# The opening of an attention-and-ReGLU kernel: chunk-wise loads of the keys' source, one form of line sums, and softmax row sums added ahead

## The chip, the cores and the metric

The kernel runs on one core of one Trainium2 chip. The metric is the device time of one execution in microseconds. Three runs of the kernel before took 1024.46, 1024.46 and 1024.63 us; their median is 1024.46 us.

## The reference, cut to what matters

```python
# q: (4, 12288, 128)   kv: (4, 384, 32, 128)   w_sr: (128, 128), all float32
kv_pool = kv.reshape(B, H // 4, 4, W // 4, 4, C).mean(axis=(2, 4))   # 4 x 4 pixels -> 1
k = v = kv_pool.reshape(B, -1, C) @ w_sr                             # 768 keys per image
s = (q @ k.transpose(0, 2, 1)) / sqrt(C)
a = exp(s - s.max(-1));  a /= a.sum(-1) + 1e-9
x = (a @ v).reshape(B * N, C)                                        # 49152 rows
out = (maximum(x @ w_gate, 0) * (x @ w_val)) @ w_out                 # d_ff = 1536
```

So each image has 768 pooled and projected keys, which are its values too, and each of the 12288 queries of an image goes through one softmax and one gated feed-forward layer. The two row-wise divisions by the softmax sum are left to the end: the feed-forward layer is of second degree in x, so its output is scaled by the inverse of the sum, squared.

## The kernel before

**Tiles.** The queries are cut into 96 tiles of 512 rows. The 768 keys of an image are six chunks of 128; two neighbouring chunks are a pair, because one row of the picture data holds both. A loaded line of a pair is a 128 x 1024 tile: 128 positions, and for each the four pixels of the even chunk and the four of the odd one, 4 KB together. Four such lines (one for each row of the 4 x 4 window) make a pair; six chunks are three pairs, 2 MB each.

**Steady part.** From the seventh tile on, one tile after another goes through the same written-out list of steps (`STEADY`): scores `s`, exponentials `e`, values `x`, value projections `v`, gate projections `g`, the gated product `h` and the output projection `o`. TensorE does s, x, v, g and o; ACT the exponentials and the copies `y` of the value projections out of PSUM; VectorE the gated products; GpSimd the output scaling. The next image's keys are prepared between these steps.

**Opening.** Image 0's keys must be made first, and meanwhile nothing of the steady kind can run. This part is a list of its own, `OPENING`, in which the order of the words is the order of issue on every engine (each engine works its own instructions off in that order). A number after `@` is the PSUM bank that a word takes. A dictionary `ENGINES` says which of ACT (a), VectorE (v) or GpSimd (p) does a word. The words that matter here:

- `a`, `b`, `c` with a chunk's number add loaded lines of a chunk (`sum_lines`, 128 x 512 fp32); the dictionary `SUMS` says which lines. `p` adds neighbouring pixels (128 x 256), `r` once more (128 x 128).
- `T3.2` transposes line 2 of chunk 3 on TensorE and adds it up in PSUM, four 128 x 128 fp32 matmuls (`turn_add`, L300); `T3.p` and `T3.r` do that with what `p` (two) or `r` (one) left. So a line may be summed on an engine ahead, or by TensorE itself.
- `kvT`, `pj`, `key`, `vt`, `val` copy the transposed chunk out, project it with w_sr (L314), keep the keys, transpose them into values (L329) and keep these.
- `cast`, `qt`, `qT` turn the first query tiles (L209). `S2.4` are the scores of tile 2 with chunk 4 (L378), `E2.4` their exponentials on ACT, `V2.4` the values (L456); `xT` keeps a finished sum of values as fp16.
- `U` with a list of chunks adds up the softmax sums of tiles 0 to 3 (`lead_sums`, L474): a matmul with ones for each tile and chunk, four tiles side by side. `R` turns these sums, `R2` inverts and squares them, `lsc` spreads them for the output scaling of `oT0`.
- `D0`, `D1` and `F384`, `F256` are matmuls whose result nobody reads; `fill(2)` at the very start is of the same kind (L663). `gate` holds GpSimd's queue until a line has landed, `W0`, `W1`, `wo` then load the weights, `ql4`, `ql5`, `qd` later queries.

**Loads before.** Pair 0's four lines go out on SP and ACT by turns, then on SP w_sr, two pairs of query tiles (512 KB each), the four lines of pair 1 and the four of pair 2. Of the eight latest loads on these two queues' shared set of semaphores, each is reused in turn: an issue waits until the load eight issues earlier has landed.

Of the kernel before, what the change touches and what calls it, by code (L numbers as in the profile page):

```python
# [16 lines left out]
def kernel(  # L17
# [33 lines left out]
    T = 512  # L51
    NS = T // 128
# [6 lines left out]
    LEAD = GRP  # L59
# [4 lines left out]
    assert NFB == 2 * NJC and NST % GRP == 0 and W // r == 8 and HC == 64  # L64

    ENGINES = dict(word.split(":") for word in """
        a0:v a1:v p0:v r0:v b1:v c1:v p1:v kvT0:v r1:p cast0:a cast1:a key0:v kvT1:v qT0:v
        cast2:a cast3:v qT1:v val0:v key1:v qT2:v qT3:v val1:a a2:v a3:v p2:p b3:v c3:v kvT2:a
        p3:p key2:a kvT3:a val2:v a5:v key3:v p5:v a4:v r5:v b4:v val3:a c4:v kvT5:a p4:v key5:v
        kvT4:a val5:v key4:v val4:v xT0:v xT2:v y0.8:v y0.2:a xT1:v y2.0:a y0.10:a cast4:p y0.7:a  # L70
        y0.6:a cast5:p y0.0:a y2.1:a xT3:a y0.1:a y1.10:a y0.5:a y0.4:a y0.3:a y0.9:a y1.8:a
        y1.1:a y1.0:a y0.11:a y1.11:v y1.3:a y2.3:a y1.7:a y1.4:a y2.2:a y2.7:a y2.4:a y1.5:a
        y1.6:a y1.2:a y2.5:v y1.9:a y2.6:a y2.11:a y2.8:a y2.9:a y2.10:a
    """.split())
    OPENING = """
        D1@2 D0@2 F384@2 a0 a1 p0 r0 T0.r@0 T0.3 b1 T0.2 c1 F256@2 p1 kvT0 r1 cast0 pj0@0 T1.r@1
        cast1 qt0@2 key0 kvT1 vt0@0 qT0 qt1@3 cast2 pj1@1 cast3 S0.0@2 qT1 qt2@4 E0.0 qt3@5 val0
        key1 qT3 S1.0@3 E1.0 vt1@1 val1 V0.0@2 S1.1@0 E1.1 S0.1@5 E0.1 qT2 S2.0@4 S2.1@1 V1.0@3
        a2 S3.1@6 V1.1 E3.1 V0.1 S3.0@5 T2.2@0 V3.1@6 p2 E2.1 a3 T2.p V2.1@1 E2.0 b3 T2.3 c3 E3.0
        U0.1@5 kvT2 pj2@0 V2.0 key2 p3 T3.p@4 kvT3 S2.2@0 E2.2 vt2@7 val2 V3.0 gate2.1 S1.2@4  # L80
        E1.2 pj3@7 a5 S0.2@0 V2.2 W0 key3 W1 ql4 ql5 S3.2@4 E0.2 E3.2 p5 V1.2 a4 S3.3@7 S0.3@0
        E3.3 V0.2 T5.2@4 E0.3 r5 T5.r vt3@7 val3 T5.3 kvT5 wo S1.3@0 S2.3@7 b4 c4 p4 V3.3 pj5@4
        V3.2 E1.3 T4.p@0 E2.3 V1.3 key5 vt5@4 S2.5@7 kvT4 val5 pj4@0 key4 E2.5 S0.5@4 E0.5 V0.3
        V2.3 S0.4@0 vt4@7 E0.4 V2.5 val4 S1.4@4 V0.5 E1.4 S2.4@7 V0.4 xT0 E2.4 S1.5@0 E1.5 S3.5@4
        V1.4 V2.4 E3.5 S3.4@7 qd3 xT2 v0.8@2 v0.2@0 E3.4 qd1 V1.5 y0.8 v0.10@4 y0.2 v2.0@1 qd0
        U2.3.4.5 xT1 y2.0 qd2 y0.10 cast4 v0.7@3 R v0.6@1 y0.7 g0.2@4 qT4 g2.0@0 h0.2 v0.0@2 y0.6
        v2.1@3 cast5 g0.7@5 h2.0 V3.5 y0.0 g0.6@4 v0.1@1 qT5 h0.7 V3.4 y2.1 v1.10@2 g0.10@0 h0.6
        xT3 o0.7@5 g0.1@3 y0.1 o0.2 h0.10 o0.6 y1.10 v0.5@4 h0.1 g0.0@1 g2.1@0 y0.5 v0.4@2 h0.0
        o0.10 y0.4 v0.3@3 g0.4@4 h2.1 o0.0 y0.3 g1.10@2 v0.9@1 h0.4 g0.5@0 y0.9 v1.8@3 h1.10 s4.0
        y1.8 o0.4 v1.1@1 h0.5 e4.0 g0.8@2 tq1 g0.9@3 h0.8 g1.8@4 v1.0@0 y1.1 o0.5 h1.8 qn1.8 s4.1  # L90
        y1.0 v1.11@2 g1.0@1 h0.9 e4.1 g0.3@4 v0.11@0 h1.0 o0.8 v1.3@3 y0.11 s4.2 y1.11 y1.3
        g1.1@1 v2.3@0 h0.3 o0.9 e4.2 g0.11@3 g2.2@2 h1.1 o0.1 y2.3 v1.7@4 o0.3 h0.11 v1.4@1 y1.7
        g1.7@0 s4.3 R2 y1.4 o0.11 h1.7 lsc e4.3 k5 g1.3@4 v2.2@1 h1.3 o1.0@3 v2.7@0 y2.2 o1.1 oT0
        o1.7 y2.7 g1.4@4 v2.4@1 h2.2 o1.3 y2.4 v1.5@0 v1.6@5 h1.4 g1.11@2 y1.5 g2.3@1 o1.8 h1.11
        y1.6 v1.2@0 g2.4@4 h2.3 s5.0 y1.2 v2.5@5 g2.6@2 h2.4 e5.0 v1.9@0 o1.10 y2.5 g2.5@1 y1.9
        g1.5@4 s5.1 h1.5 o1.4 e5.1 g1.2@0 v2.6@5 h2.5 g1.6@4 o1.11 y2.6 o1.5 h1.6 v2.11@1 s5.2
        h1.2 y2.11 o1.6 g2.7@4 e5.2 v2.8@5 h2.6 v2.9@0 g1.9@1 h2.7 o1.2 y2.8 g2.8@2 s5.3 h1.9
        y2.9 v2.10@5 g2.9@4 e5.3 h2.8 g2.11@0 o1.9 g2.10@1 h2.9 y2.10 oT1 h2.10 h2.11
    """.split()
    LAST = [f"{head}{n}" for n in range(NFB) for head in "ovygh"] + ["oT"]  # L100
    DRAIN = """
# [43 lines left out]
    def engine_of(name):  # L145
        return {"a": nc.scalar, "v": nc.vector, "p": nc.gpsimd}[ENGINES.get(name, "a")]
# [32 lines left out]
    def q_load_pair(i):
        q32 = work.tile([128, 2, NS, C], FP32, tag="kv_s2", bufs=2, name="q32")  # L180
        nc.sync.dma_start(
            q32, q[0, i * T : (i + 2) * T, :].rearrange("(p i s) c -> p i s c", i=2, s=NS)
        )
        for n in range(2):
            q32s[i + n] = q32[:, n]
# [40 lines left out]
    kv16 = const.tile([128, B, NJC, 2 * C + 16], FP16)  # L226
    kv_in = {}

    def kv_load(b, pair, lines=range(r), queues=(nc.sync,)):
# [12 lines left out]
        rows = kv[b, pair * 2 * HC : (pair + 1) * 2 * HC].rearrange(  # L242
            "(hp dh) (wp h dw) c -> dh hp wp (h dw c)", dh=r, h=2, dw=r
        )
        for dh in lines:
            queues[dh % len(queues)].dma_start(  # L246
                parts[dh].rearrange("p h dw c -> p (h dw c)"), rows[dh]
            )

    s3s, kv_Ts, key_banks = {}, {}, {}  # L250
# [15 lines left out]
    def line(chunk, dh):  # L266
        return kv_in[0, chunk // 2][dh][:, chunk % 2]

    sums, pixels = {}, {}

    def add(name, to, x, y):
        engine_of(name).tensor_tensor(to, x, y, op=ALU.add)  # L272
# [98 lines left out]
    aTs, x_banks, x16s, xTs, rinvs = {}, {}, {}, {}, {}  # L371
# [93 lines left out]
    sums_left = [NJC]  # L465

    def lead_sums(chunks):
        for jc in chunks:
            first = "sums" not in x_banks
            if first:  # L470
                x_banks["sums"] = bank([128, T])
            sums_left[0] -= 1
            for k in range(LEAD):
                nc.tensor.matmul(  # L474
                    x_banks["sums"][32 * k : 32 * (k + 1), :], ones, aTs[k][:, jc, :],
                    start=first, stop=sums_left[0] == 0, skip_group_check=True,
                    tile_position=(0, 32 * k),
                )

# [155 lines left out]
    ones = const.tile([128, 32], FP16)  # L635
# [40 lines left out]
    gate = const.tile([128, 1], FP32)  # L676

    def open_step(word):
        head = "T" if word[0] == "T" else word.rstrip("0123456789.")
        at = [int(x) for x in word[len(head):].split(".") if x] if head != "T" else []  # L680
        if head in ("a", "b", "c"):
            j = at[0]
            x, y = SUMS[j][head]
# [34 lines left out]
        elif head == "xT":  # L718
            lead_kept(word, at[0])
        elif head == "U":  # L720
            lead_sums(at)
        elif head == "R":
            lead_inverse() if at else lead_sums_turned()
        elif head == "lsc":
# [11 lines left out]
        elif head == "D":  # L736
# [3 lines left out]
                start=True, stop=True,  # L740
# [3 lines left out]
            nc.gpsimd.dma_start(wv16[:, own], moe_w_val[:, own])  # L744
            nc.gpsimd.dma_start(wg16[:, own], moe_w_gate[:, own])
        elif head == "gate":
            nc.gpsimd.tensor_copy(gate, line(2 * at[0], at[1])[:, 0, 0:1])
        elif head == "ql":
            q_load_tile(at[0])
        elif head == "wo":  # L750
# [1 line left out]
        elif head == "qd":  # L752
            q_tiles(1)
            rows = q[0, GRP * T : 2 * GRP * T, :].rearrange(
                "(i t j s) c -> j t i s c", i=GRP, t=32, s=NS
            )
# [12 lines left out]
        elif head == "o":  # L769
            k, n = at[0], o_left.get(at[0], NFB)  # L770
# [137 lines left out]
```

## Time and profile before

| what | before |
|---|---|
| median of three runs | 1024.46 us (1024.46 to 1024.63) |
| span of the profiled execution, first to last instruction | 1022.5 us |
| median time less that span | 1.96 us |
| TensorE (PE) busy | 1017.2 us, 99% |
| ACT busy | 918.5 us, 90% |
| VectorE (DVE) busy | 869.4 us, 85% |
| GpSimd (POOL) busy | 524.0 us, 51% |
| mean granted TensorE clock | 1.000 |

The profile has no time of its own for the profiled execution but the span: its own time is taken as the span with the 1.96 us around it. Rows of a timeline read: start, duration (for several merged instructions, from the first start to the last end), engine, line of the kernel, operation, tile written and tile read, shapes, count, and in brackets the idle time before it with what ended it. Rows of groups read: line, engine, operation, count, then total busy time and mean duration in ns, then the idle time before. A matmul's row includes its drain; the next one starts before it ends. Rows of stretches give the length, then busy time and count for PE, its weight loads, DVE, ACT and POOL, then the granted clock, the DMA share and GB/s.

### The profile page before, as it was taken

Reading aid. Unit: us, or ns where it says so; the run is one execution under the profiler, and the core shown is the slowest. Engines: PE = TensorE matmul, PEld = TensorE weight load, DVE = VectorE, ACT = ScalarE, POOL = GpSimd, SP = SyncE. Lnnn points to the kernel's source line nnn. Section 1 sums busy time; section 2 is a strip of 40 time slices with the busy share of each in tenths; the row PEclk is TensorE's granted clock in tenths of the full one; section 3 lists DMA queues with packets and bytes.
Section 4 is the critical chain, followed back from the end, with each engine's and each line's share of the span. In section 5 each row is a group of like instructions: output and inputs, shape, how many; then the busy total and the mean of one; then the engine's idle time right before and its main releaser. Section 6 shows DMA issues by size and latency. Waiting matters only on the chain.

```text
span 1022.5 us, 17480 instructions
## 1 busy us (share of the span) xinstructions
PE 1017.2 (99%) x5021; PEld 485.2 (47%) x5021; DVE 869.4 (85%) x1450; ACT 918.5 (90%) x1927; POOL 524.0 (51%) x1312
## 2 busy tenths in 40 slices
PE   9999999999999999999999999999999999999998
PEld 4444444444444444444444444444444444444445
DVE  5988888888888888888888888888888888888888
ACT  5999998999999999999999999999999999999986
POOL 3487857344437576544434856754434543443342
PEclk9999999999999999999999999999999999999999
DMA  9999999878799999868779999978787878777651
GB/s 317 172 171 184 186 211 145 140 122 132 132 198 156 201 164 184 136 116 143 125 134 201 165 186 187 157 131 137 128 130 114 147 122 129 124 119 124 98 91 44
DMA packets 475743, 153.48 MB, mean 150 GB/s; under 512 B 451584, under 2 KB 465920, under 8 KB 475648
## 3 DMA queue, kind: packets, MB, share of 16 engines
q1 hardware_dynamic: 453184, 126.08, 65.9%
q0 software_dynamic: 22032, 25.19, 17.6%
q10 hardware_dynamic: 432, 1.11, 0.3%
q8 instruction: 39, 0.64, 0.3%
q14 instruction: 56, 0.46, 0.2%
HBM read 53.94 MB, written 26.35 MB: 79 GB/s over the span
## 4 chain that ended last, share of the span: by engine, by line
PE 99%; DMA 1%; DVE 0%; ACTq 0%; issue 0%
PE bank_ps L504 24%; PE bank_ps L515 24%; PE bank_ps L545 24%; PE wide_ps L397 12%; PE bank_ps L439 12%; PE bank_ps L529 1%; DMA kv_in<-in_kv_dram 1%; PE bank_ps L456 1%; PE bank_ps L378 1%; PE wide_ps L336 0%; PE bank_ps L300 0%; PE bank_ps L314 0%; PE bank_ps L474 0%; DVE kv_s L272 0%; PE bank_ps L209 0%; ACTq L246 0%
## 5 line engine op out<-in xcount | busy, mean ns | idle before, releaser
L523 DVE SCALAR_TENSOR_TENSOR hT<-bank_ps,val 128x512 f16<-128x512 f32 x1152 | 727.3, 679 | 104.4 <-PE bank_ps L515 83.7
L141 ACT CAST val<-bank_ps 128x512 f16<-128x512 f32 x1149 | 628.4, 596 | 44.4 <-PE bank_ps L504 23.9
L504 PE MATMUL bank_ps<-xT,wv 128*128 128x512 f16 x1152 | 421.0, 379 | 0.0
L515 PE MATMUL bank_ps<-xT,wg 128*128 128x512 f16 x1152 | 376.3, 379 | 0.0
L545 PE MATMUL bank_ps<-hT,wo 128*128 128x512 f16 x1116 | 348.7, 379 | 0.0
L402 ACT ACTIVATE a<-wide_ps 128x768 f16<-128x768 f32 x368 | 302.2, 821 | 44.0 <-PE wide_ps L397 44.0
L397 PE MATMUL wide_ps<-kv,qT 128*128 128x512 f16 x736 | 179.8, 326 | 0.0
L439 PE MATMUL bank_ps<-aT,kv 128*128 128x512 f16 x552 | 179.0, 379 | 0.0
L558 POOL TENSOR_TENSOR o_sb<-o_t,scale 128x512 f32<-128x512 f32 x89 | 93.2, 1047 | 158.8 <-issue 141.0
L545 PEld LDWEIGHTS <-wo 128*128 128x128 f16 x1116 | 109.1, 98 | 132.1 <-issue 0.5
L515 PEld LDWEIGHTS <-wg 128*128 128x128 f16 x1152 | 112.6, 98 | 122.5 <-issue 0.2
L504 PEld LDWEIGHTS <-wv 128*128 128x128 f16 x1152 | 112.5, 98 | 105.4 <-issue 0.4
L423 POOL COPY scale<-square 32x8 f32<-32x8 f32 x736 | 141.2, 192 | 28.6
L416 POOL TENSOR_TENSOR square<-inverse 128x8 f32<-128x8 f32 x46 | 9.3, 202 | 248.9 <-DVE inverse L414 248.9
L838 POOL DMA_DIRECT2D out_dram<-o_sb x208 | 130.3, 632 | 9.6 <-POOL o_sb L558 7.4
L397 PEld LDWEIGHTS <-qT 128*128 128x128 f16 x736 | 71.9, 98 | 87.0 <-issue 0.2
L447 DVE CAST xT<-bank_ps 128x512 f16<-128x512 f32 x92 | 63.6, 691 | 31.7 <-PE bank_ps L439 31.6
L439 PEld LDWEIGHTS <-kv 128*128 128x128 f16 x552 | 53.9, 98 | 65.2
L402 ACT ACTIVATION_READ_ACCUMULATOR a<-wide_ps 128x1 f32 x368 | 76.1, 207 | 0.0
L553 DVE STREAM_TRANSPOSE o_t<-bank_ps 128x512 f32<-128x512 f32 x93 | 65.4, 703 | 0.3 <-PE bank_ps L504 0.2
L162 POOL DMA_DIRECT2D q<-in_q_dram x84 | 48.8, 581 | 0.3 <-issue 0.3
L256 POOL TENSOR_TENSOR s<-kv_in 128x512 f32<-128x512 f32 x36 | 45.1, 1281 | 0.7
(86 smaller groups left out, 210.8 us busy)
## 6 DMA issues: line engine op xcount, KB each, us to landing
kv_in<-in_kv_dram SPq DMA_DIRECT2D x42, 512.0 KB, 5.3
out_dram<-o_sb SPq DMA_DIRECT2D x177, 64.0 KB, 3.6
q<-in_q_dram POOLq DMA_DIRECT2D x88, 128.0 KB, 3.4
out_dram<-o_sb POOLq DMA_DIRECT2D x176, 64.0 KB, 4.2
aT<-a SPq DMA_TRANSPOSE x184, 4.5
kv_line<-in_kv_dram SPq DMA_DIRECT2D x4, 512.0 KB, 9.8
placed<-blocks SPq DMA_DIRECT2D x9, 128.0 KB, 2.5
kvT<-placed SPq DMA_DIRECT2D x36, 32.0 KB, 2.2
```

The costliest lines, as they stand in the source:

```text
L141: nc.scalar.copy(to, what)
L397: nc.tensor.matmul(s_ps[:, j0 * 128 : j1 * 128], qT, kv16[:, b, j0:j1, 0:C], start=True, stop=True)
L402: nc.scalar.activation(a16s[k][:, s, :], s_banks.pop(s)[:, 0:J], AF.Exp, scale=qk_scale, accum_out=a_sums[k // 2][:, k % 2, s : s + 1],)
L423: nc.gpsimd.tensor_copy(to[32 * b : 32 * (b + 1), :, :, j], squares[k // 2][32 * j : 32 * (j + 1)])
L439: nc.tensor.matmul(x_banks[k], kv16[:, k // NST, jc, C : 2 * C], aT[:, jc], start=first, stop=x_left[k] == 0,)
L504: nc.tensor.matmul(proj_banks["v", k, fb], wv16[:, fb * 128 : (fb + 1) * 128], xTs[k], start=True, stop=True,)
L515: nc.tensor.matmul(proj_banks["g", k, fb], wg16[:, fb * 128 : (fb + 1) * 128], xTs[k], start=True, stop=True,)
L523: nc.vector.scalar_tensor_tensor(hTs[k][:, fb, :], freed(proj_banks.pop(("g", k, fb))), 0.0, vals.pop((k, fb)), op0=ALU.max, op1=ALU.mult,)
L545: nc.tensor.matmul(o_banks[k], wo16[:, fb, :], hTs[k][:, fb, :], start=first, stop=o_left[k] == 0)
L553: nc.vector.transpose(o_t, freed(o_banks.pop(k)))
L558: nc.gpsimd.tensor_tensor(to, o_by, scale.to_broadcast([128, NS, 4, 32]), op=ALU.mult)
L838: queue.dma_start(*out_moves.pop())
```

## The change

1. **Loads.** A list `LOADS` takes the place of the six calls. Pair 0, w_sr and the first queries keep their queues and their order (of the two queues, ACT's first issue now stands first). Chunks 2, 3, 5 and 4 are then loaded one after the other, line by line, each line of a chunk by its own DMA: 128 pieces of 2 KB, 256 KB. `kv_load` gets a parameter `halves` for it.
2. **Line sums.** `SUMS` is the same for all six chunks: `a` adds lines 0 and 1, `b` adds line 2, TensorE transposes the sums' pixels (`T.p`) and the raw line 3 (`T.3`). The words `c` and `r` are gone.
3. **Row sums.** New words `m` (`m2.1`: for tile 2, chunk 2 + chunk 3) and `n` (`n2.1.2`: pair 1 + pair 2) add the fp16 exponentials ahead, six `m` on VectorE, six `m` and four `n` on GpSimd. `U6.7` then takes only two summed tiles for each of the four query tiles: eight matmuls instead of 24.
4. **The list.** `OPENING` and `ENGINES` are new throughout. `D0`, `F384` and `F256` are left out; three of the first four query casts move from ACT to GpSimd; `a1` and `a5` are done on GpSimd, the other sums and all `p` on VectorE; of the copies `xT`, two instead of three are done on VectorE; the turn of the sums (`R`) stands next to `R2`, some 95 words later than before.

```diff
-        D1@2 D0@2 F384@2 a0 a1 p0 r0 T0.r@0 T0.3 b1 T0.2 c1 F256@2 p1 kvT0 r1 cast0 pj0@0 T1.r@1
-        cast1 qt0@2 key0 kvT1 vt0@0 qT0 qt1@3 cast2 pj1@1 cast3 S0.0@2 qT1 qt2@4 E0.0 qt3@5 val0
...
-        U2.3.4.5 xT1 y2.0 qd2 y0.10 cast4 v0.7@3 R v0.6@1 y0.7 g0.2@4 qT4 g2.0@0 h0.2 v0.0@2 y0.6
+        a1 a0 cast1 b1 b0 p1 cast0 T0.3@2 D1@0 T1.3@7 p0 cast2 T1.p T0.p qt1@1 kvT0 qT1 kvT1 qt0@4
+        pj1@6 cast3 pj0@3 qt2@5 key1 qt3@1 S1.1@0 key0 vt1@2 S1.0@7 qT0 vt0@6 a2 qT2 b2 p2 qT3 val1
...
+        S3.3@2 b4 p4 ql4 V0.0 kvT5 val3 E3.3 V0.2 pj5@3 T4.3@0 T4.p V2.3 ql5 key5 S0.5@2 m3.1 vt5@3
+        kvT4 pj4@5 m0.1 val5 key4 S2.5@0 wo V1.3 V0.3 S0.4@3 m1.1 vt4@5 E0.5 V0.5 qd1 E2.5 S2.4@2
+        m2.0 E0.4 S1.5@0 val4 S3.5@5 V0.4 S1.4@3 V2.5 E2.4 qd2 m1.0 V2.4 E1.5 xT0 S3.4@2 xT2 V1.5
+        v0.2@0 qd0 v0.10@1 E1.4 E3.5 V1.4 v0.8@3 V3.3 g0.2@7 v2.0@5 y0.2 qd3 y0.8 v0.7@0 E3.4 m0.2
...
+        U6.7@2 e4.1 h0.11 v2.3@1 qn1.8 y1.1 v1.11@3 h1.0 R R2 o0.11 g2.2@5 y2.3 tq1 s4.2 v2.7@0
...
-    SUMS = [{"a": [1, 0]}, {"a": [1, 0], "b": ["s", 3], "c": ["s", 2]}, {"a": [0, 1]}, {"a": [0, 1], "b": ["s", 2], "c": ["s", 3]}, {"a": [0, 1], "b": ["s", 2], "c": ["s", 3]}, {"a": [0, 1]}]
+    LOADS = """
+        p0l1:a p0l0 p0l3:a p0l2 w Q0 Q2 c2l0 c2l1 c2l2 c2l3 c3l0 c3l1 c3l2 c3l3 c5l0 c5l1 c5l2 c5l3
+        c4l0 c4l1 c4l2 c4l3
+    """.split()
+    SUMS = [
+        {"a": [0, 1], "b": ["s", 2]},
...
+    ]
...
-                parts[dh].rearrange("p h dw c -> p (h dw c)"), rows[dh]
+                parts[dh][:, halves].rearrange("p h dw c -> p (h dw c)"),
+                rows[dh].rearrange("hp wp (h x) -> hp wp h x", h=2)[:, :, halves].rearrange(
+                    "hp wp h x -> hp wp (h x)"
+                ),
...
+    def pair_of(k, n):
+        if n not in a_pairs:
+            a_pairs[n] = work.tile(
+                [128, LEAD, T], FP16, tag="kv_s2" if n else "a_pair", bufs=2 if n else 1, name="a_pair"
+            )
+        return a_pairs[n][:, k]
+
+    def add_chunks(name, k, n):
+        add(name, pair_of(k, n), aTs[k][:, 2 * n], aTs[k][:, 2 * n + 1])
+
+    def add_pairs(name, k, n, m):
+        add(name, pair_of(k, n), pair_of(k, n), pair_of(k, m))
...
-    kv_load(0, 0, range(r), (nc.sync, nc.scalar))
-    nc.sync.dma_start(w_sr_f32, w_sr)
-    q_load_pair(0)
-    q_load_pair(2)
-    kv_load(0, 1)
-    kv_load(0, 2)
+    for word in LOADS:
...
+            if word[0] == "p":
+                kv_load(0, n, [dh], (queue,))
+            else:
+                kv_load(0, n // 2, [dh], (queue,), slice(n % 2, n % 2 + 1))
```

More of the change, by code (lines that the diff above doesn't have):

```diff
@@ L66 @@
     ENGINES = dict(word.split(":") for word in """
[L67 to L71, printed above, removed]
@@ L72 @@
-        y1.1:a y1.0:a y0.11:a y1.11:v y1.3:a y2.3:a y1.7:a y1.4:a y2.2:a y2.7:a y2.4:a y1.5:a
-        y1.6:a y1.2:a y2.5:v y1.9:a y2.6:a y2.11:a y2.8:a y2.9:a y2.10:a
+        a1:p a0:v cast1:p b1:v b0:v p1:v cast0:p p0:v cast2:p kvT0:a qT1:v kvT1:a cast3:v key1:a
+        key0:a qT0:v a2:v qT2:a b2:v p2:v qT3:v val1:a val0:a a5:p kvT2:v a3:v key2:v b3:v p3:v
+        kvT3:a val2:v key3:v m3.0:v b5:v p5:v a4:v b4:v p4:v kvT5:a val3:v key5:a m3.1:v kvT4:a
+        m0.1:v val5:v key4:v m1.1:v m2.0:v val4:v m1.0:v xT0:v xT2:v y0.2:v y0.8:v m0.2:p xT1:a
@@ L89 @@
[L89 to L94, printed above, removed]
@@ L177, in q_turn_two, with q_load_pair @@
             del q16s[g]
[L179 to L185, printed above, removed]
+    def q_load_pair(i, parts=slice(0, 2)):
+        if i not in q32_pairs:
+            q32_pairs[i] = work.tile([128, 2, NS, C], FP32, tag="kv_s2", bufs=2, name="q32")
+        rows = q[0, i * T : (i + 2) * T, :].rearrange("(p i s) c -> p i s c", i=2, s=NS)
+        nc.sync.dma_start(q32_pairs[i][:, parts], rows[:, parts])
+        for n in range(parts.start, parts.stop):
+            q32s[i + n] = q32_pairs[i][:, n]
     def q_load_tile(i):
@@ L227, with kv_load @@
     kv_in = {}
-    def kv_load(b, pair, lines=range(r), queues=(nc.sync,)):
+    def kv_load(b, pair, lines=range(r), queues=(nc.sync,), halves=slice(0, 2)):
         if (b, pair) not in kv_in:
@@ L471, in lead_sums @@
                 x_banks["sums"] = bank([128, T])
-            sums_left[0] -= 1
             for k in range(LEAD):
                 nc.tensor.matmul(
-                    x_banks["sums"][32 * k : 32 * (k + 1), :], ones, aTs[k][:, jc, :],
-                    start=first, stop=sums_left[0] == 0, skip_group_check=True,
+                    x_banks["sums"][32 * k : 32 * (k + 1), :], ones,
+                    aTs[k][:, jc, :] if jc < NJC else pair_of(k, jc - NJC),
+                    start=first, stop=last and jc == chunks[-1], skip_group_check=True,
                     tile_position=(0, 32 * k),
@@ L746, in open_step @@
         elif head == "gate":
-            nc.gpsimd.tensor_copy(gate, line(2 * at[0], at[1])[:, 0, 0:1])
+            nc.gpsimd.tensor_copy(gate, line(*at)[:, 0, 0:1])
         elif head == "ql":
```

65 lines of the change are left out of this document (47 added, 18 removed).

## The prediction

> **What bounds the kernel now.** I read the page first (engine shares, the chain that ended last), then the table of stretches, then the opening row by row.
>
> ```profile
> span 1022.5 us, 17480 instructions
> PE 1017.2 (99%) x5021; PEld 485.2 (47%) x5021; DVE 869.4 (85%) x1450; ACT 918.5 (90%) x1927; POOL 524.0 (51%) x1312
> PE 99%; DMA 1%; DVE 0%; ACTq 0%; issue 0%
> 8.30:12.70 4.40, 3.82 (x35) 3.01 (x35) 3.56 (x11) 1.98 (x4) 0.45 (x1) 1.00 1.04 421
> 12.70:27.70 15.00, 15.00 (x92) 7.84 (x90) 9.72 (x22) 13.05 (x30) 7.46 (x14) 1.00 1.06 301
> 200.00:400.00 200.00, 199.99 (x965) 94.57 (x964) 170.81 (x283) 182.66 (x386) 105.43 (x266) 1.00 0.91 162
> ```
>
> The first number after a stretch is its length, the second TensorE's busy time. TensorE is the bound from 12.7 us to the end, and 99% of the chain lies on it. The change touches only the opening list; from the late part of it on, the instruction streams of all engines are the same. So it can move the end only by TensorE work that it removes or adds in the first 45 us, and by TensorE waits that it opens or closes there. The stretch 8.3 to 12.7 is the one with visible idle time (0.6 us). Its rows, with those of the row sums (L474) and the first value projection (27.74):
>
> ```profile
> 1.37 3.78 PE L663 MATMUL bank_ps<-ident 128*128 128x512 f32 x4 [1.37 <-POOL ident masks.py:199]
> 5.01 2.46 PE L738 MATMUL bank_ps<-kv_in,ident 128*128 128x512 f32 x4
> 7.52 0.91 PE L672 MATMUL bank_ps<-ident 128*128 128x384 f32 x2
> 8.33 0.33 PE L300 MATMUL bank_ps<-ident,kv_c 128*128 128x128 f32 x1
> 8.51 1.09 PE L300 MATMUL bank_ps<-ident,kv_in 128*128 128x128 f32 x8
> 9.44 0.60 PE L672 MATMUL bank_ps<-ident 128*128 128x256 f32 x2
> 10.62 0.49 PE L314 MATMUL bank_ps<-kvT_chunk,w_sr_f 128*128 128x128 f32 x2 [0.58 <-DVE kvT_chunk L143]
> 12.28 0.61 PE L209 MATMUL bank_ps<-ident,q 128*128 128x128 f16 x8
> 12.72 0.38 PE L378 MATMUL bank_ps<-qT,kv 128*128 128x512 f16 x1
> 13.02 0.23 PE L329 MATMUL bank_ps<-ident,kv 128*128 128x128 f16 x1
> 17.24 0.61 PE L474 MATMUL bank_ps<-aT,ones 128*32 128x512 f16 x8
> 27.74 0.59 PE L504 MATMUL bank_ps<-xT,wv 128*128 128x512 f16 x2
> 28.91 1.05 PE L474 MATMUL bank_ps<-aT,ones 128*32 128x512 f16 x16
> ```
>
> Work before 8.3 is filler (L663, L738, L672): no result of it is used. A 512-column fp16 matmul advances TensorE by 0.22 us (two take 0.59, one 0.38).
>
> **TensorE work removed and added.** Row sums go from 24 matmuls (0.61 + 1.05 us) to 8 (0.61): -1.05. Chunk transposes go from 33 to 36, each 0.11 (of 8, 1.09 less the 0.2 of the last one's drain): +0.33. Fillers dropped lie in waits and count nothing by themselves. Sum: -0.7 us.
>
> **The start.** Lines of pair 0 and the first q pairs keep their queues and order. Their arrival, by who waited for it or by issue plus time to landing:
>
> ```profile
> 6.32 1.29 DVE L272 TENSOR_TENSOR kv_s<-kv_in 128x512 f32<-128x512 f32 x2 [5.41 <-DMA kv_in<-in_kv_dram]
> 8.49 1.42 DVE L272 TENSOR_TENSOR kv_s<-kv_s,kv_in 128x512 f32<-128x512 f32 x2 [0.21 <-DMA kv_in<-in_kv_dram]
> L246 SPq DMA_DIRECT2D kv_in<-in_kv_dram x1: 818/818/818, 1.5 to 1.5; - x1
> DMA to landing us min/median/max: 7.3/7.3/7.3
> 10.23 1.90 ACT L141 CAST q<-q 128x512 f16<-128x512 f32 x3 [6.57 <-DMA q<-in_q_dram]
> 14.91 1.04 POOL L272 TENSOR_TENSOR kv_c<-kv_s 128x256 f32<-128x256 f32 x1 [4.01 <-PE bank_ps L378]
> 17.54 0.72 POOL L272 TENSOR_TENSOR kv_c<-kv_s 128x256 f32<-128x256 f32 x1 [1.58 <-DVE kv_s L272]
> 15.42 1.08 DVE L272 TENSOR_TENSOR kv_s<-kv_s,kv_in 128x512 f32<-128x512 f32 x1
> 16.70 0.69 DVE L272 TENSOR_TENSOR kv_s<-kv_s,kv_in 128x512 f32<-128x512 f32 x1 [0.20 <-DMA kv_in<-in_kv_dram]
> ```
>
> Lines 0 and 1 are there at 6.3, line 3 at 8.5, line 2 at 8.8 (1.5 + 7.3), q from 10.2. The last four rows show a collision: the GpSimd add at 14.91 and the VectorE add at 15.42 each take 0.3 to 0.4 us more than the same operation without an overlap. The new start puts line 0+1 of chunk 1 and three q casts on GpSimd beside VectorE adds, so I charge one such collision.
>
> Chain after: b1 waits for line 2, 8.8 to 9.5; b0, p1 to 10.45; p0 loses 0.6 to the cast on GpSimd, to 11.4; its two transposes to 11.65, seen at 11.85; two kvT copies on ACT (0.27 + 0.2) to 12.3; two projections (0.5) and two q transposes (0.45) to 13.3. There the first score S1.1 starts. In before the second score starts at 12.72. At those two points the new list has done two transposes more (0.22) and a score and a value transpose less (0.28): 0.06 less done. So Delta = (13.3 - 12.72) - 0.7 + 0.06, which is -0.05, if TensorE then waits as long as before.
>
> **The loads.** Chunks 2, 3, 5, 4 come in 16 issues of 256 KB instead of 8 of 512 KB. Before:
>
> ```profile
> 14.07 1.29 DVE L272 TENSOR_TENSOR kv_s<-kv_in 128x512 f32<-128x512 f32 x2 [0.39 <-DMA kv_in<-in_kv_dram]
> 19.22 0.19 POOL L747 COPY gate<-kv_line 128x1 f32<-128x1 f32 x1 [0.96 <-DMA kv_line<-in_kv_dram]
> L246 SPq DMA_DIRECT2D kv_line<-in_kv_dram x1: 535/535/535, 11.5 to 11.5; - x1
> DMA to landing us min/median/max: 10.2/10.2/10.2
> DMA packets 677, 2.45 MB, mean 408 GB/s; under 512 B 80, under 2 KB 80, under 8 KB 677
> DMA packets 231, 0.41 MB, mean 412 GB/s; under 512 B 29, under 2 KB 145, under 8 KB 231
> ```
>
> From the second line of pair 1 (14.05) to that of pair 2 (19.2) are four lines: 1.28 us each; the last lands at 21.7 (11.5 + 10.2). An issue costs SP 0.54 us, less than the 0.64 that half a line takes, so SP keeps up. The price of 2 KB pieces is not shown. The last two rows are 13 to 19 us (4 KB pieces) and 8 to 9 us (116 pieces of 512 B and 86 of 4 KB): the 0.06 MB in 512 B pieces took the 0.16 us that 4 KB pieces left, an estimated 370 GB/s. So bounds: no loss, or 10% (+1.1 us); the fixed part per piece shrinks fourfold from 512 B to 2 KB, so I take 4%: last landing 22.2. Chunk 4's last line is needed by T4.3. Behind it, up to the first value projection, stand 6 transposes, a projection, two value transposes and 16 scores and values: 4.6 us, so 26.8 against 27.74 before. Nobody waits; cover 0.9 us. Nor below nothing: TensorE is full in 12.7 to 27.7, so earlier data alone wins only the small waits. Those came to some 0.8 us there (44 scores and values 9.5, 23 transposes 2.9, 4 projections 1.1, 5 value transposes 0.3, row sums 0.5, in 15.0). I take 0.3 of it as won: Delta -0.35.
>
> On GpSimd, the first-half add a5, the gate and the weights' issue come 0.5 us later (19.7); value projections need the first weights at 27.7, and those landed by then with over 3 us to spare. SP's later transposes and stores keep their relative places but for one transpose of q placed ahead of tile 4's second a-transpose, needed only at k = 6 (some 60 us): cover of 8 us.
>
> **Row sums added ahead.** Six adds go to VectorE, ten to GpSimd, before the eight row-sum matmuls.
>
> ```profile
> L256 POOL TENSOR_TENSOR s<-kv_in 128x512 f32<-128x512 f32 x36 | 45.1, 1281 | 0.7
> L558 POOL TENSOR_TENSOR o_sb<-o_t,scale 128x512 f32<-128x512 f32 x89 | 93.2, 1047 | 158.8 <-issue 141.0 <-DVE o_t L553 14.5 <-DMA aT<-a 3.3
> L143 POOL CAST q<-q_late 128x512 f16<-128x512 f32 x2 | 1.2, 609 | 6.4 <-DMA q_late<-in_q_dram 6.4
> L143 DVE COPY qT<-bank_ps 128x512 f16<-128x512 f16 x4 | 1.6, 419 | 0.0
> ```
>
> No fp16 add of two tiles is shown on either engine. VectorE: between 0.42 (fp16 copy) and 0.69 (fp32 add); I take 0.42, as half the bytes. At 0.69 the score S3.5 would wait for val4 behind m1.1 and m2.0, +0.5. The Trainium skill ("VectorE: DVE Perf Modes", What auto-detection actually checks) lets a 16-bit two-source op run two elements per cycle; no run here shows it, and by it the sum stays as it is.
>
> GpSimd: between 0.61 (one-input cast) and 1.28; I take 1.25, the two-input rows. The chain starts when E0.4 is done, about 25.9, and its ten adds and two late q casts (0.6 each) end 13.7 us later, at 39.6. TensorE reaches U6.7 53 matmuls after the first projection (11.5 us): 27.6 + 11.5 = 39.1, the last group 0.2 later. It waits 0.3, and a shift of the whole opening moves both alike; behind the wait stand s4.2 and all projections. At 1.05 per add nothing waits; at 1.5 it waits 2.8. Taken: +0.3. Moving xT1 from VectorE to ACT and the turn of the sums to later only takes load off VectorE. Delta: -0.05.
>
> **The clock.** The fillers D0, F384 and F256 go. Of the four fp32 passes from 1.37, each took 0.9 us; from 5.0 0.6; the 256-column ones at 9.44 0.22 apiece (0.44 per 512). So TensorE started at half speed and was at full speed by 8.5, and TensorE was never idle in between. In the new list it stops at 5.0 and next has work at 8.5: 3.4 us idle. At the end of the run:
>
> ```profile
> 1016.42 2.84 PE L529 MATMUL bank_ps<-wo,hT 128*128 128x128 f16 x48
> 1000.00:1023.00 23.00, 19.26 (x195) 12.90 (x193) 18.29 (x31) 14.14 (x28) 5.43 (x9) 0.99 0.17 46
> ```
>
> The last matmul ends at 1019.3 and the mean granted clock of that stretch is 0.99, so it fell before 1023, some 3 us after. I take a halved clock from about 8.7 to 12.2 as likelier than not: T0.3, D1, T1.3 and T1.p (2.0 us at full speed) take twice that, of which 1.0 us was waiting for p0 anyway: +0.8. Delta +0.75.
>
> The Trainium skill ("TensorE: Matmul & The Clock Gate", What's actually happening) says that the clock halves after an idle window of about 3.4 us and is full again after a busy one, with windows that run freely; that speaks against this change. The early and the last rows here agree with it, but where the windows fall no row shows.
>
> **Sum.** -0.7 work, +0.65 start, -0.3 small waits, +0.3 row sums, +0.8 clock = +0.75. The span becomes 1023.25; around the span lie 1.96 us (1024.46 - 1022.5), which the change doesn't touch. Predicted 1025.2.
>
> **Rivals.** (1) Slower: the clock stays halved for two windows, to about 15.6, because the opening's transposes and waits don't count as busy. Then 12.2 to 15.6 loses another 1.7: 1026.9. For: half of what TensorE does until 12.2 are transposes and waits. Against: D1, a true matmul, stands in between. It decides if a 512-column matmul after 13 us still takes over 0.4 us to the next. (2) GpSimd late: fp16 adds at 1.5 (collisions as at 14.91): +2.5 beyond the sum, 1027.7; visible as a TensorE wait before L502. Against: GpSimd's neighbours then are gating operations with one operand in PSUM, beside which L256 kept 1.28. (3) 2 KB pieces far slower, 35% (beyond any rate shown): last landing 25.3; the forecast has T4.3 at 28.4 - 4.6 = 23.8, so +1.5: 1026.7. It decides from a landing of 23.8 on, 20%. (4) The clock doesn't fall: 1024.4, and with GpSimd at 1.05 1024.1; with all small waits gone too 1023.6. (5) The loads don't arrive by chunk (each issue waits for the landing of the one eight before it): they end where they did and the start alone counts; 1025.2 again, so it changes nothing.
>
> **How the numbers follow.** 0.2% (2.05 us) is about what a measurement of this kernel can tell from no change. Chances: forecast 0.42, (1) 0.18, (2) 0.08, (3) 0.04, (4) 0.24, (5) 0.04. (1), (2) and (3) end over 1026.5: slower 0.30. Faster by 2.05 needs (4), all small waits gone and a start that is 1.2 us earlier than worked out above: 0.06 of its 0.24. Within: 0.42 + 0.18 + 0.04 = 0.64. Range: down to the low end of (4) at 1023.6, up to (2) at 1027.7, which takes in (1) with its rough price; left out are the faster end of (4) and two of the slow cases together.
>
> **What would show it.** Right: TensorE idle 5.0 to 8.5, fp32 transposes at 0.21 apart until about 12.2, S1.1 near 14, the first wv matmul near 28.4, U near 39.9 with a short wait for GpSimd; last kv_line landing near 22.2. Wrong: transposes at 0.11 apart from 8.5; a wait over 1 us before L502; GpSimd adds at 0.7 or 1.6; kv_line landing after 23.

## The result, and the profile after

The changed kernel took 1030.64 us (median of five runs, 1027.92 to 1031.42), the kernel before in the same comparison 1024.63 us: a ratio of 1.0052, with a 95% interval of 1.0039 to 1.0064. Ratio and interval are worked out from all runs and not from the two medians, so they can differ a little from the difference of these. By the medians it is slower by 6.0 us, by the ratio by 5.3, where 1025.2 (1023.6 to 1027.7) was predicted. The profiled execution has a span of 1027.3 us against 1022.5, 4.8 us more; it took 1029.58 us, so it is one of the shorter runs.

The page of the changed kernel:

```profile
span 1027.3 us, 17464 instructions
...
PE 1015.1 (99%) x5002; PEld 486.8 (47%) x5002; DVE 870.4 (85%) x1449; ACT 917.5 (89%) x1929; POOL 538.3 (52%) x1324
...
PE 97%; DMA 2%; DVE 1%; ACT 0%; issue 0%; ACTq 0%
```

TensorE has less to do than before, 1015.1 instead of 1017.2 us, and yet the end is later, so TensorE waits more. The chain now holds 2% of DMA, where it held 1%. The table of stretches (length, then TensorE's busy time) says where:

```profile
5.00:8.30 3.30, 0.15 (x1) 0.00 (x0) 0.69 (x1) 0.00 (x0) 1.76 (x1) 1.00 1.03 414
8.30:12.70 4.40, 4.14 (x14) 3.00 (x15) 2.38 (x4) 0.00 (x0) 2.03 (x3) 1.00 1.04 407
...
60.00:75.00 15.00, 13.53 (x66) 6.24 (x65) 12.23 (x21) 12.24 (x27) 14.52 (x34) 1.00 1.12 192
...
100.00:120.00 20.00, 18.01 (x87) 8.32 (x86) 15.22 (x26) 16.28 (x36) 16.89 (x39) 1.00 1.16 217
```

The prediction looked at the first two. The last two lie in the steady part, far behind the changed list, and there TensorE stands idle for 1.5 and 2.0 us. TensorE's rows of these two waits in the timeline of after, and the same two matmuls (the first value matmuls of tiles 5 and 9) in before:

```profile
72.88 0.39 PE L455 MATMUL bank_ps<-aT,kv 128*128 128x512 f16 x1 [1.47 <-DMA aT<-a]
...
116.50 0.38 PE L455 MATMUL bank_ps<-aT,kv 128*128 128x512 f16 x1 [1.99 <-DMA aT<-a]
```

```profile
70.01 0.38 PE L439 MATMUL bank_ps<-aT,kv 128*128 128x512 f16 x1
...
111.47 0.38 PE L439 MATMUL bank_ps<-aT,kv 128*128 128x512 f16 x1
```

In after both wait for `aT<-a`: the transpose of a tile's exponentials, a DMA that SP issues in two halves per tile (`a_turn`). In before neither waits. These 3.46 us are most of the 4.8. The other 1.3 us come from the opening: tile 4's first value matmul, the last landmark ahead of these waits, starts at 60.88 us in after and at 59.64 in before, 1.2 us later. Both have to be explained.

**The late transpose.** SP's queue in after, from the timeline:

```profile
44.42 1.35 SPq L811 DMA_TRANSPOSE qT<-q  x1
...
50.97 1.97 SPq L445 DMA_TRANSPOSE aT<-a  x1
59.03 0.84 SPq L819 DMA_DIRECT2D out_dram<-o_sb  x2
59.92 0.54 SPq L259 DMA_DIRECT2D kv_in<-in_kv_dram  x1
60.50 1.54 SPq L819 DMA_DIRECT2D out_dram<-o_sb  x3
62.15 2.11 SPq L445 DMA_TRANSPOSE aT<-a  x1
64.31 2.08 SPq L819 DMA_DIRECT2D out_dram<-o_sb  x3
66.43 0.56 SPq L259 DMA_DIRECT2D kv_in<-in_kv_dram  x1
67.09 1.58 SPq L445 DMA_TRANSPOSE aT<-a  x1
```

The transpose for which TensorE waits at 72.88 is the one issued at 67.09; it lands 5.7 us later. Tile 5's exponentials had ended at 54.1 (53.25 and 0.82), so this issue stands 13 us after its data were there. From 59.03 on SP issues one transfer after the other: 7.67 of the 8.06 us up to 67.09 are issue time. The wait at 116.50 is of the same kind: that transpose is issued at 110.19, 14.8 us after tile 9's exponentials ended (95.39), and lands 6.2 us later; in before it goes out 9.2 us after them (101.66 and 92.50) and lands 4 us ahead of its use. From 59.03 to that point SP's rows show no pause over 0.6 us. Ahead of 59.03 is a hole from 52.94, and the waits of SP's queue (engine and line, what it waited for; us, times, longest) name it:

```profile
SPq L819 <- POOL o_sb L587: 6.0, 1, 6.0
```

SP waited 6.0 us for GpSimd's first output scaling (L587). GpSimd's timeline of after, and then of before:

```profile
40.87 2.21 POOL L175 DMA_DIRECT2D q<-in_q_dram  x4 [0.18 <-PE bank_ps L544]
53.14 1.08 POOL L175 DMA_DIRECT2D q<-in_q_dram  x2 [10.06 <-DMA qT<-q]
54.21 3.67 POOL L525 COPY lead_scale<-lead_square 32x16 f32<-32x16 f32 x16
57.95 1.05 POOL L587 TENSOR_TENSOR o_sb<-o_t,lead_scale 128x512 f32<-128x512 f32 x1
```

```profile
42.66 3.65 POOL L496 COPY lead_scale<-lead_square 32x16 f32<-32x16 f32 x16 [1.24 <-DVE lead_square L491]
46.25 1.07 POOL L162 DMA_DIRECT2D q<-in_q_dram  x2
47.39 1.04 POOL L558 TENSOR_TENSOR o_sb<-o_t,lead_scale 128x512 f32<-128x512 f32 x1
```

Here is the cause. The 16 copies (`lsc`, L525) and the two query loads (`k5`, L175) have changed places in GpSimd's queue. The loads overwrite a buffer that the transpose `tq1` (L811) reads, so they wait for its landing. In before `tq1` was issued at 34.60 and landed 5.1 us later, so the loads, with the copies ahead of them, found nothing to wait for:

```profile
34.60 1.42 SPq L766 DMA_TRANSPOSE qT<-q  x1
```

In after the word `tq1` stands behind `e4.1`, so SP issues it only at 44.42, behind tile 4's first a-transpose (`e4.1` ends the first half of that tile's exponentials), and it lands 8.0 us later. GpSimd stands 10.06 us, with the copies, which need nothing of these loads, queued behind; the first scaling ends at 59.0 instead of 48.4; SP stands behind the scaling, and all later transposes behind SP.

The chain of waits alone would mislead here. Around the first wait it reads:

```profile
66.46 0.63 ACT val L154 x2
67.09 5.74 DMA aT<-a
...
72.88 0.39 PE bank_ps L455
```

It follows the transpose back to a copy on ACT that ends at the same moment, and shows none of SP's issues. Only SP's own rows show that the transpose came at that moment because its queue had come to it.

**The start.** TensorE's rows of after:

```profile
8.56 1.11 PE L316 MATMUL bank_ps<-ident,kv_in 128*128 128x128 f32 x4 [3.41 <-DMA kv_in<-in_kv_dram]
...
12.03 1.06 PE L316 MATMUL bank_ps<-ident,kv_c 128*128 128x128 f32 x4
12.88 1.06 PE L222 MATMUL bank_ps<-ident,q 128*128 128x128 f16 x8
...
14.41 0.61 PE L222 MATMUL bank_ps<-ident,q 128*128 128x128 f16 x8
14.86 0.38 PE L394 MATMUL bank_ps<-qT,kv 128*128 128x512 f16 x1
...
20.35 0.44 PE L316 MATMUL bank_ps<-ident,kv_c 128*128 128x128 f32 x2 [0.69 <-DVE kv_c L288]
...
29.46 0.59 PE L533 MATMUL bank_ps<-xT,wv 128*128 128x512 f16 x2
...
40.77 0.62 PE L502 MATMUL bank_ps<-a_pair,ones 128*32 128x512 f16 x8
```

After 3.4 us without work TensorE runs at half speed: eight fp16 transposes take 1.06 us from 12.88, and 0.61 us from 14.41. So the clock is back only near 14, and the first score is at 14.86.

### The profile page after: what moved, and what is told of

The parts are those of the page before. It is cut to its first block, busy times and chain, and to the rows that moved or that the text cites. A ratio compares the mean times of both kernels' runs of the same rounds, so it can differ in the third digit from the quotient of the medians.

```text
span 1027.3 us, 17464 instructions
## 1 busy us (share of the span) xinstructions
PE 1015.1 (99%) x5002; PEld 486.8 (47%) x5002; DVE 870.4 (85%) x1449; ACT 917.5 (89%) x1929; POOL 538.3 (52%) x1324
## 4 chain that ended last, share of the span: by engine, by line
PE 97%; DMA 2%; DVE 1%; ACT 0%; issue 0%; ACTq 0%
PE bank_ps L533 24%; PE bank_ps L544 24%; PE bank_ps L574 23%; PE bank_ps L455 12%; PE wide_ps L413 11%; DMA aT<-a 1%; PE bank_ps L558 1%; DMA kv_in<-in_kv_dram 1%; PE bank_ps L316 1%; PE bank_ps L394 0%; PE bank_ps L472 0%; PE wide_ps L352 0%; DVE hT L552 0%; ACT a L418 0%; PE bank_ps L783 0%; PE bank_ps L330 0%
## 5 line engine op out<-in xcount | busy, mean ns | idle before, releaser
L587 POOL TENSOR_TENSOR o_sb<-o_t,scale 128x512 f32<-128x512 f32 x89 | 93.2, 1048 | 158.5 <-issue 141.4
L175 POOL DMA_DIRECT2D q<-in_q_dram x84 | 48.8, 582 | 10.2 <-DMA qT<-q 10.1
```

The lines of the kernel that those rows point to most:

```text
L587: nc.gpsimd.tensor_tensor(to, o_by, scale.to_broadcast([128, NS, 4, 32]), op=ALU.mult)
```

## The experiments

**Theory A**: the 10 us wait on GpSimd, through SP's queue, makes the a-transposes late. Its rival, **theory B**: the transposes are late because they meet the next image's loads, which come at other moments than before. **Theory C**: the start is late because the clock fell while TensorE was idle. Its rival: the start waits for VectorE's sums. Each kernel was timed against the kernel before on the same chip; "over before" is the difference of the two medians, to be compared with +6.0 us for the change as it is.

**lsc alone moved back ahead of k5** in the changed kernel:

```diff
-        g1.2@1 k5 o0.8
+        g1.2@1 lsc k5 o0.8
...
-        y1.7 lsc h1.2
+        y1.7 h1.2
```

> The changed kernel with one word moved: lsc (16 copies on GpSimd that spread the inverse sums) stands ahead of k5 (two query loads on GpSimd) again, as before. Theory A (GpSimd's queue delays SP's): the copies run at about 43 to 47 us instead of 54.2 to 57.9; the two query loads still wait for tq1's transpose until 52.5; the first output scaling ends near 55.3 instead of 59.0; SP's wait for it falls from 6.0 to about 2.3 us; tile 5's second transpose lands near 69 instead of 72.8; TensorE's waits of 1.47 us at 72.9 and 1.99 us at 116.5 are gone. Time 3 to 4.5 us below the changed kernel: about 1026.5. Theory B (the transposes are late because they meet the next image's loads, whatever SP waited for before): both waits stay within 0.5 us of what they were, time 1029 to 1031.

Measured: 1025.85 us, 1.6 over before (ratio 1.0019, interval 1.0010 to 1.0029). Nothing of the steady part waits any more in the profiled execution; SP waits 0.5 us for the scaling. But that execution took 1024.34 us and is the second shortest of eleven; single runs go up to 1029.64, and what waits in those no trace shows. So by the medians 4.4 of the 6.0 us are gone with one word, as theory A has it (3 to 4.5). Theory B would have kept 1029 to 1031; it falls, here and in the next two runs.

**tq1 alone moved back behind e4.0**, with lsc still behind k5:

```diff
-        y2.3 tq1 s4.2
+        y2.3 s4.2
...
-        h0.3 e4.0 y2.2
+        h0.3 e4.0 tq1 y2.2
```

> The changed kernel with one word moved: tq1 (a transpose of queries on SP's queue) stands right behind e4.0, ahead of tile 4's first a-transpose, as before; lsc stays behind k5. Theory A: the transpose is issued near 36.6 instead of 44.4 us and lands near 42, so the two query loads of k5 no longer hold GpSimd; lsc runs from 44.2 to 47.9, the first output scaling ends near 49 and SP does not wait for it. Both late waits of TensorE are gone, with more slack than when lsc alone is moved: time 1026 to 1026.5. If the wait of GpSimd is not what tq1 sets: the wait on GpSimd ahead of the two loads stays near 10 us and the time near 1030. Theory B: 1029 to 1031.

Measured: 1024.44 us, 0.2 over before (1.0003, 0.9994 to 1.0011). GpSimd's rows of this kernel:

```profile
40.82 3.29 POOL L175 DMA_DIRECT2D q<-in_q_dram  x6 [0.16 <-issue]
44.10 3.70 POOL L525 COPY lead_scale<-lead_square 32x16 f32<-32x16 f32 x16
47.87 1.05 POOL L587 TENSOR_TENSOR o_sb<-o_t,lead_scale 128x512 f32<-128x512 f32 x1
```

The two loads now follow the four before them at once, the copies start at 44.10 as expected, and SP has no wait for the scaling. The time is better than the 1026 expected. By the medians the late queues cost 5.8 us (5.0 by the ratios). Between the two profiled executions it is 3.8 us (spans of 1027.3 and 1023.5), near the 3.5 us of the two waits, and their openings are alike: tile 4's first value matmul starts at 60.88 and 60.83.

**k5 alone moved back behind e4.3**, so behind lsc, and behind tile 4's second a-transpose on SP, with tq1 as late as in the change:

```diff
-        g1.2@1 k5 o0.8
+        g1.2@1 o0.8
...
-        h1.7 e4.3 g1.4@0
+        h1.7 e4.3 k5 g1.4@0
```

> The changed kernel with one word moved: k5 (a transpose of queries on SP, two query loads on GpSimd) stands behind e4.3, as before, so behind lsc and behind tile 4's second a-transpose in its two queues; tq1 stays late. Theory A (the order of the two queues is the cause, not how late tq1's transpose itself is): lsc runs from about 43 to 47, the first output scaling follows without waiting for the loads, tile 4's second transpose is issued right at the end of its exponentials (46.4 instead of 51.0), SP does not wait 6.0 us; slack of tile 5 and of tile 9 over 2.5 us, no late wait of TensorE: 1024.3 to 1025. If the late tq1 alone is enough: waits of 1 us or more stay and the time is 1026 to 1030.

Measured: 1025.56 us, 1.2 over before (1.0010, 1.0001 to 1.0018), with no late wait in the profiled execution. So it is not the late tq1 by itself that costs the 5.8 us, but that two loads which wait for it stand ahead of work that SP needs. The time came out 0.5 us above what was expected. What is left fits the slow start, which this kernel keeps: in its profiled execution, 1025.44 us, tile 4's first value matmul starts at 60.53 us, 0.9 later than in before, and TensorE has no wait behind that. Tile 9's second half landed only 0.9 us before its use there, so a short wait in some other runs is possible; none was seen.

**The same fault in the kernel before**: tq1 from behind e4.0 to behind e4.1, lsc from ahead of k5 to behind it, and nothing else.

```diff
-        g0.8@2 tq1 g0.9@3
+        g0.8@2 g0.9@3
...
-        h0.9 e4.1 g0.3@4
+        h0.9 e4.1 tq1 g0.3@4
...
-        h1.7 lsc e4.3 k5
+        h1.7 e4.3 k5 lsc
```

> The kernel before with only two words moved: tq1 goes from behind e4.0 to behind e4.1, lsc from ahead of k5 to behind it. Theory A: GpSimd waits for tq1's transpose with lsc queued behind it, the first output scaling and SP's queue come late by 4 to 8 us, tile 5's and tile 9's second transposes (4.4 and 4.1 us of slack now) come late: waits of TensorE of 1 to 4 us in all, time 1025.5 to 1028.5. Theory B, or a slack that is enough: no wait of TensorE over 0.3 us, 1024.5.

Measured: 1025.12 us, 0.9 over before (1.0012, 1.0002 to 1.0023), single runs up to 1030.19. The mechanism is there:

```profile
50.02 1.08 POOL L162 DMA_DIRECT2D q<-in_q_dram  x2 [8.54 <-DMA qT<-q]
...
112.62 0.38 PE L439 MATMUL bank_ps<-aT,kv 128*128 128x512 f16 x1 [0.77 <-DMA aT<-a]
```

GpSimd waits 8.5 us, SP 5.0, and TensorE 0.77 us at tile 9. The median is below the expected 1025.5 to 1028.5. SP is less late than in the change: the first scaling ends at 55.9 us instead of 59.0, and tile 5's second transpose goes out at 63.88 instead of 67.09. That `k5` stands behind tile 4's second a-transpose here, which goes out at 44.94 instead of 50.97, is not shown to be the reason: with tq1 early it goes out at 51.98, and nothing waits.

**The fillers put back** at the head of the changed kernel's list:

```diff
-        a1 a0 cast1 b1
+        D1@6 D0@6 F384@6 a1 a0 cast1 b1
```

> The changed kernel with fillers D1, D0 and F384 put at the head of the list, so that TensorE works from 5.0 to about 8.4 us. Theory C (the start is late because the clock fell in the idle 5.0 to 8.5): transposes of T0.3 0.11 us apart instead of 0.22, full clock to the end, the first score at 13.3 to 13.6 instead of 14.86, the first value projection near 28.3 instead of 29.46; 1.2 us less, if the late waits of 1.5 and 2.0 us stay. Rival (the start waits for the sums of pair 0 on VectorE, done at 11.34): the first score at 14.5 to 14.9, no gain.

Measured: 1028.71 us (1.0038, 1.0026 to 1.0050), 4.5 over before, so by the medians 1.5 us less than the change alone; the two intervals overlap, so the trace has to decide. The first score is at 13.04 instead of 14.86 and the first value projection at 26.97 instead of 29.46, earlier than expected. But not all of these 2.5 us reach the end: with the whole opening earlier and SP's queue unchanged, the late waits grow to 4.2 us. The row of transposes below is at full speed, eight in 0.61 us, where the change took 1.06.

```profile
11.36 0.61 PE L222 MATMUL bank_ps<-ident,q 128*128 128x128 f16 x8
...
70.86 0.39 PE L455 MATMUL bank_ps<-aT,kv 128*128 128x512 f16 x1 [1.94 <-DMA aT<-a]
...
103.73 0.39 PE L455 MATMUL bank_ps<-aT,kv 128*128 128x512 f16 x1 [1.60 <-DMA aT<-a]
...
114.94 0.38 PE L455 MATMUL bank_ps<-aT,kv 128*128 128x512 f16 x1 [0.68 <-DMA aT<-a]
```

**The fillers taken from the kernel before** (D1 stays):

```diff
-        D1@2 D0@2 F384@2 a0
+        D1@2 a0
...
-        c1 F256@2 p1
+        c1 p1
```

> The kernel before without the fillers D0, F384 and F256 (D1 stays). TensorE then has no work from 6.2 to about 8.3 us and stands again while pixel sums are made. Theory C: the clock is halved from some point before 8.5 to 12 or 14 us, the first score is later by 0.5 to 1.5 us and the time 1024.7 to 1025.7. If the fillers did not hold the clock: 1024.2, no change.

Measured: 1025.87 us, 1.6 over before (1.0014, 1.0005 to 1.0023), a little over the range expected. Its first score is at 13.35 us instead of 12.06, and the eight fp32 transposes, 1.09 us in before, take nearly twice that:

```profile
8.48 0.44 PE L300 MATMUL bank_ps<-ident,kv_c 128*128 128x128 f32 x1 [2.31 <-DVE kv_c L272]
8.72 1.96 PE L300 MATMUL bank_ps<-ident,kv_in 128*128 128x128 f32 x8
```

Together with the run above theory C stands by the traces. What the matmuls whose result nobody reads are worth in time is 1.5 to 1.6 us by the medians of these two runs.

**The three edits together** (tq1 early, lsc ahead of k5, fillers at the head; the diffs are those above):

> The changed kernel with three edits: tq1 behind e4.0, lsc ahead of k5, and the fillers D1, D0, F384 at the head. Tile 4's values start at 59.64 us in before, at 60.8 with tq1 moved and at 58.39 with the fillers alone. Theories A and C add up: tile 4's values near 58.4, no late wait of TensorE over 0.3 us, so 1.2 us below before: about 1023.0, faster than both kernels by what the opening itself saves. If with an earlier start the transposes of tiles 5 to 9 have no slack again: a late wait comes back and the time is 1024 to 1026.

Measured: 1023.58 us, 0.7 below before by the medians and 0.3 by the ratio (0.9997, 0.9987 to 1.0006), where 1023.0 was expected; the interval holds no change. There is no late wait in the profiled execution, but one of the eleven runs took 1028.00 us. Against tq1 early alone it is 0.9 us less. With these in place, the parts of the change could be priced without the noise of the late waits:

**Row sums as 24 matmuls again**, on top of the three edits, all words m and n left out:

```diff
-        U6.7@2 e4.1
+        U0.1.2.3.4.5@2 e4.1
...
-        E0.2 m3.0 b5
+        E0.2 b5
```

> The three edits, and the row sums as 24 matmuls at the place of the eight, without the words m and n. The prediction's terms: 16 matmuls more cost 1.05 us of TensorE, a wait for GpSimd of up to 0.3 us goes: 0.75 to 1.05 us above the three edits alone. If adding ahead saved nothing (VectorE and GpSimd held up TensorE elsewhere for as long), the two are equal within 0.3 us.

Measured: 1024.47 us (1.0003, 0.9994 to 1.0012), 0.9 over the three edits by the medians. The intervals of the two overlap, but the rows agree: from the first row sum to the next matmul behind the group takes 0.54 us with eight, 1.41 us with 24, and tile 4's first value matmul starts at 59.41 instead of 58.54.

```profile
38.44 0.61 PE L502 MATMUL bank_ps<-a_pair,ones 128*32 128x512 f16 x8
38.98 0.60 PE L533 MATMUL bank_ps<-xT,wv 128*128 128x512 f16 x2
```

```profile
38.45 1.48 PE L502 MATMUL bank_ps<-aT,ones 128*32 128x512 f16 x24
39.86 0.61 PE L533 MATMUL bank_ps<-xT,wv 128*128 128x512 f16 x2
```

**Pairs of 4 KB lines again** in place of chunk-wise 2 KB pieces, on top of the three edits:

```diff
-        p0l1:a p0l0 p0l3:a p0l2 w Q0 Q2 c2l0 c2l1 c2l2 c2l3 c3l0 c3l1 c3l2 c3l3 c5l0 c5l1 c5l2 c5l3
-        c4l0 c4l1 c4l2 c4l3
+        p0l1:a p0l0 p0l3:a p0l2 w Q0 Q2 p1l0 p1l1 p1l2 p1l3
+        p2l0 p2l1 p2l2 p2l3
```

> The three edits, with pairs 1 and 2 loaded line by line in 4 KB pieces as before. If the pieces' size costs as predicted (4%), the last line lands at 21.7 instead of 22.35 us. But chunk 2's last line then lands near 16.6 instead of 14.3, chunk 3's with it: the list, which asks for chunk 2 at 16.3, would wait 1 to 1.5 us there, and the time is 0.3 (the prediction's gain from chunk-wise loads) to 1.5 us above the three edits alone. If the order of arrival is hidden: equal or up to 0.5 us below.

Measured: 1026.52 us (1.0022, 1.0013 to 1.0031), 2.9 over the three edits, twice the top of what was expected. TensorE waits at chunk 2 for the line and at chunk 3 for the sums that follow from it:

```profile
16.63 0.63 PE L316 MATMUL bank_ps<-ident,kv_in 128*128 128x128 f32 x4 [1.91 <-DMA kv_in<-in_kv_dram]
...
20.82 0.44 PE L316 MATMUL bank_ps<-ident,kv_c 128*128 128x128 f32 x2 [0.77 <-DVE kv_c L288]
```

So within this list the order of arrival matters. It is no price of chunk-wise loads as such, since the list is written for them: the kernel before, with its own list, takes 1024.25 us in this comparison with pairs. What the 2 KB pieces would do to its list was not tried.

**The three edits with k5 late as well**, lsc where the three edits have it:

```diff
-        g1.2@1 lsc k5 o0.8
+        g1.2@1 lsc o0.8
...
-        h1.7 e4.3 g1.4@0
+        h1.7 e4.3 k5 g1.4@0
```

> The three edits (tq1 early, lsc early, fillers), with k5 behind e4.3 as well. Theory A: tile 5's slack grows from 2.4 to 4 us or more, tile 9's from 2.6 to about 4; TensorE has no late wait in either, so the time is that of the three edits, 1023.2 to 1023.7, with fewer single runs above it. If the moved transpose then misses tile 6: a wait there, over 1024.

Measured: 1023.63 us, 0.8 below before (0.9993, 0.9984 to 1.0002), and all runs between 1023.45 and 1023.95, where those of the change spread over 3.5 us. It is the steadiest version found. Its median is under that of before, but the interval still holds no change, so no version here is shown to be faster than the kernel before.

## Why the prediction was wrong

**The step that failed** is in the paragraph on the loads: "SP's later transposes and stores keep their relative places but for one transpose of q placed ahead of tile 4's second a-transpose, needed only at k = 6 (some 60 us): cover of 8 us." Two words of the new list were not followed through their queues. With it falls the sentence near the start that the change can move the end only by TensorE's work and waits in the first 45 us: the two waits that it opened stand at 72.9 and 116.5. `k5` issues a transpose on SP and also two loads on GpSimd, and those stand ahead of `lsc` now. And `tq1` stands behind `e4.1`, so behind an a-transpose for which SP itself waits until 41.4. That the turn of the sums stands later did not fail: with tq1 early it stands as late, and the copies that follow it start at 44.10 without a wait. The cover was read for one transpose, 8 us before its use; what came was a shift of the whole queue, and SP, which issues almost without a pause from 59.03 on, cannot make up for it. Priced by the runs: 5.8 us by the medians (the change 6.0 over before, with tq1 early 0.2), 3.8 us between the two profiled executions. No rival had it; rival (2) is the nearest, GpSimd late, but by its adds and in front of L502.

**The start.** At full clock the first score was put at 13.3; with the fillers it came between 13.04 and 13.20. The halved clock was taken as likelier than not, and "S1.1 near 14" was 14.86, because the clock came back near 14 and not at 12.2, about half way to rival (1). The term of 0.8 us for it was too small: by the medians the fillers are worth 1.5 us in the change, where the late waits grow by 0.7 us with them, 1.6 in the kernel before, and 0.9 between tq1 early and the three edits; in the profiles of the change without and with them, the first value projection moves by 2.5 us. The Trainium skill ("TensorE: Matmul & The Clock Gate", What's actually happening) has the windows of the clock run freely; the profiled kernels without fillers have their first score at 14.21, 14.46, 14.73 and 14.86, which fits, and the one with the change's queues put right (tq1 early) spreads over 2.1 us from run to run, the one with the fillers too and k5 late over 0.5 us. The idle window of about 3.4 us that the same section gives is longer than what was needed here: in the kernel before without fillers the transposes are slow after a wait of only 2.31 us.

**Row sums.** -1.05 us of TensorE and +0.3 for GpSimd made -0.75; measured -0.9. That the two are near is in part luck, as both terms were off and in opposite ways: by the rows the 16 matmuls less are worth 0.87 us and not 1.05, which counted the last matmul's drain of a whole group as time saved, and the wait was not 0.3. The unknown prices: an fp16 add on VectorE was taken at 0.42, one on GpSimd at 1.25.

```profile
L288 DVE TENSOR_TENSOR a_pair<-aT 128x512 f16<-128x512 f16 x6 | 2.3, 416 | 0.0
...
L288 POOL TENSOR_TENSOR a_pair<-aT 128x512 f16<-128x512 f16 x6 | 6.8, 1142 | 2.3 <-issue 2.3
```

They are 0.416 and 1.14 us. The rule of the Trainium skill ("VectorE: DVE Perf Modes", What auto-detection actually checks) on 16-bit operands that the prediction weighed holds here: the fp32 add of as many elements takes 0.69. TensorE waited next to nothing for U6.7: the matmul before it starts at 40.47 and one advances by 0.22, so it waited 0.08 us.

**The loads.** The last line was issued at 17.0 and landed 5.3 us later, at 22.35; 22.2 was predicted, from 4% for the smaller pieces. The 0.3 us of small waits that earlier chunks were to save were not seen in the change as it is: a wait of 0.69 us for p3's pixel sums stands at 20.35 instead. That wait is not there with the three edits.

**The sum.** The terms that were worked out come to -0.7 us in the runs with the queues and the clock put right (1023.58 against 1024.25), and -0.05 was predicted for them (+0.75 less 0.8 for the clock). The interval of that run, -1.3 to +0.6 us, holds both, so it confirms no single term. For the change with its queues right and its slow start (tq1 early), the forecast of +0.75 met +0.2, and the interval, -0.6 to +1.1 us, holds it. The parts that the prediction worked out were read about right. What it missed is what two moved words do to two queues.

## What to carry to other kernels

When a list of steps is reordered, write out for each queue what each moved word issues there, DMAs included, and ask of the first instruction that can wait what stands behind it: a load that waits for a buffer should not stand ahead of work that is ready. Slack of a transfer has to be compared with the shift of its whole queue, not with the delay of one instruction, and a queue that issues nearly without a pause gives a delay on for many tiles: here for 60 us, over two waits. A single profiled execution may show less of this than the runs do, so the spread of the runs belongs to the reading.

## What the runs showed of the hardware that was not expected

The column of the granted clock says 1.00 for 8.3 to 12.7 us in after, while the same matmuls there take twice their time; in a short stretch at the start the spacing of equal matmuls (eight fp16 transposes in 1.06 or 0.61 us) tells the clock and the column does not. When full speed comes back differs between executions with the same instructions up to there: in the run with lsc moved four fp32 transposes take 0.60 us from 12.10 on, in the change 1.06 us from 12.03 on. And how long one transpose of the same size takes to land varies widely within an execution: 3.8 us for the one issued at 115.67 in after, 9.0 us for the one issued at 104.87. Whether this is what spreads the runs of the changed kernel over 3.5 us, and why its late queue cost 3.5 us in the profiled execution but 5.8 us by the medians, was not tested.
